# One more tile of a fused attention and feed-forward kernel takes its first products by a seven-product block scheme

## The chip, the cores and the metric

The kernel runs on one core of one Trainium2 chip. The metric is device time in microseconds (us), the median of several executions. A core has five engines that work side by side, each through its own list of instructions: PE (matmul; PEld is its weight load), DVE (vector), ACT (scalar), POOL (GpSimd) and SP (which here only issues DMAs). Engines wait for one another through semaphores.

## The reference

```
r = maximum(x, 0); phi(x) = concat(r * cos, r * sin)      # q and k, position s of 576
kv = k_p^T v;  z = sum_s k_p;  attn = (q_p kv) / (q_p z + 1e-6)     # 8 batches, 8 heads, D = 64
x = attn as (4608, 512)
h = ((x @ w1) * (x @ w2)) @ w3                              # w1, w2: 512 x 1024
out = h @ w_out                                              # 4608 x 512
```

The kernel first forms w3 @ w_out once (`w34b`, 1024 x 512), so each tile of x needs x @ w1, x @ w2, their product abT and abT @ w34b.

## The kernel before

Attention runs by batch b (0 to 7) and chunk c (0 to 4: four of 128 positions, one of 64). The feed-forward runs by tile t (0 to 8) of 512 tokens; a tile's `xT` is filled by DMA transposes of finished chunks. What stands where is written out by hand in `PLAN`: each line is split at its semicolons and the steps are issued in that order, so every engine's instruction order follows from it. The steps that matter here:

- `f t`: the next piece of tile t's products (generator `ffn_groups`, L700, or `fast_units`, L832); `o t`: the next piece of abT @ w34b of a tile in `FAST`.
- `n b c`: the eight matmuls of a chunk's numerator and denominator (L603); `d b c`: its division on DVE (a reciprocal, L624, and a product, L625), into a tile `xblk`; `xd b c`: the DMA transpose on SP's queue that takes `xblk` to `xT`.
- `q`, `k b c n`: features, the cosine part on DVE (L517), the sine part for n heads on ACT (L522) and the rest on DVE (L525); `qd b c`: the DMA transpose of q's features, on SP's queue; `v b c`: a copy on DVE, ACT or POOL; `kv b`: 40 matmuls; `l`, `lg`, `lx`: loads, the last two gated.
- `tf i`: weight sum i; `xs t i`: sum i of blocks of x (L830); `h t p`: the product of two finished blocks (L889); `s t i`: sum i of blocks of abT (L1007).

Three ways lead through a tile. Tiles 0 and 1 do eight block products in both stages. Tiles in `SEVEN` (2 to 6) form x @ w1 and x @ w2 plainly, 64 matmuls of 256 columns and 32 of 512 on PE, copy one of the two on ACT (`asb`) and multiply on DVE (L762, L778); then abT @ w34b comes in seven chained block products (`seven_products`, L1009). Tiles in `FAST` (7 and 8) take x @ w1 and x @ w2 too by seven chained block products, since [w1 w2] is a 2 x 2 block matrix W11 W12 / W21 W22: 112 matmuls of 256 columns, with sums t1 to t4 of the weights and s1 to s4 of the tile. Each of four column groups then needs four copies on ACT (L862, L866, L869, L876) and three operations on DVE (L872, L880, L883), and two products more make the second half (L889):

```
for p, m in ((0, 4), (0, 2), (0, 5), (1, 1), (0, 3), (1, 6), (1, 7), (1, 2), (1, 4), (1, 5), (1, 3)):
    step(p, m)
    yield
```

Product 7 takes t3 and s3, product 6 t2 and s2, product 4 t4, product 3 s4. A product that is added to a bank waits for the copy or sum that reads the bank before it. The seven products of the second stage are chained in the same way: the block sums L1026 and the copies L1029 read a bank before it is written on.

Of the kernel before, what the change touches and what calls it, by code (L numbers as in the profile page):

```python
# [137 lines left out]
f 3; q 5 0 0; lx 6 q 0; lg 6 q 1; k 5 3 8
f 3; n 4 2; lg 6 k 0; xd 3 2; d 4 2 A; l 6 k 1; l 6 v 1; xd 3 3; q 5 1 4; xd 4 0; xd 4 1; xd 4 2
f 3  # L140
f 3; q 5 3 8
# [4 lines left out]
f 4
f 3; n 4 3; k 5 2 8; k 5 0 0; qd 5 0
f 4
f 3; q 5 4 0; qd 5 4; v 6 0 G; d 4 3 A
f 4; v 6 1 G  # L150
f 4; lx 7 k 0
f 4; n 4 4
# [2 lines left out]
f 4; xd 4 3
f 4; q 5 2 8; d 4 4 V; qd 5 1; qd 5 3
f 4; kv 5
f 4; qd 5 2; n 5 0; xd 4 4; k 6 0 0; d 5 0 V; lg 7 k 1; n 5 4; v 6 3 A
# [89 lines left out]
f 8
f 8
f 8; h 8 0 V; s 8 3 V  # L250
f 8
f 8
f 8; h 8 1 V
o 8
f 8; s 8 2 V; s 8 4 V; s 8 1 V; ss; ss
o 8
# [66 lines left out]
def kernel(  # L323
# [483 lines left out]
    W11, W12, W21, W22 = (w[:, ts(r, 2), :] for r in range(2) for w in (w1b, w2b))

    def ffn_weight_sum(i, on):

# [2 lines left out]
        on.tensor_tensor(out=out, in0=a, in1=b, op=ALU.subtract)
# [7 lines left out]
    def x_sum(t, i, on):

        if t not in xsums:
            flat = va_bufs[t % 2 ^ 1][:].rearrange("p c h e -> p (c h e)")
# [5 lines left out]
        on.tensor_tensor(out=out, in0=a, in1=b, op=op)  # L830

    def fast_units(t):  # L832

        (s1, s2, s3, s4), (t1, t2, t3, t4) = xsums[t], wsum
# [7 lines left out]
        (m7, u1), (c11, c21, c22) = spare["f32"], spare["bf16"]  # L842
        x, y, z = {}, {}, {}

        def product(into, u, m, first=True):
            w, a = factors[m]
            for i in range(2):
                for kc in range(2):
                    nc.tensor.matmul(into[:, ts(i, 256)], lhsT=w[:, kc, ts(2 * u + i, 128)], rhs=a[:, kc, :],  # L849
                                     start=(first and i == 0 and kc == 0), stop=(i == 1 and kc == 1),  # L850
                                     skip_group_check=not first)

        def step(p, m, js=(0, 1)):
            if m == 1:
                for bank in (x, y):
                    for j in range(2):
                        bank[2 * p + j] = keep_bank()
            for j in js:
                u = 2 * p + j
                if m == 1:  # L860
                    product(x[u], u, 1)
                    nc.scalar.copy(out=y[u][:, :], in_=x[u][:, :])  # L862
                elif m == 7:
# [2 lines left out]
                    nc.scalar.copy(out=m7[:, j], in_=z[u][:, :])  # L866
                elif m == 6:
                    product(x[u], u, 6, False)
                    nc.scalar.copy(out=u1[:, j], in_=x[u][:, :])  # L869
                elif m == 4:  # L870
# [1 line left out]
                    nc.vector.tensor_tensor(out=c21[:, j], in0=z[u][:, :], in1=u1[:, j], op=ALU.add)  # L872
# [337 lines left out]
```

## Time and profile before

| | |
|---|---|
| median of 3 runs | 241.46 us (240.49 to 241.84) |
| profiled execution, its own time | 240.19 us |
| its span, first to last instruction | 238.4 us |
| mean granted clock of PE | 1.000 |
| POOL busy | 83.1 us, 35% of the span |

The span is what the profile's times count from (0 to 238.4); some 1.8 us of the execution's time lie outside it. "Busy" is the time in which an engine had an instruction at work. In the timeline each row gives start, length, engine, line of the program, operation, what is written and read, and in brackets how long the engine had sat idle and who released it. A matmul row lasts longer than the step to the next one, since matmuls overlap; the step from start to start is what a matmul costs.

### The profile page before, as it was taken

How to read it: one execution, taken by the hardware profiler on the slowest of the kernel's cores; microseconds unless marked ns; L12 is line 12 of the kernel's file. 1: busy time of each engine (PE TensorE's matmuls, PEld its weight loads, DVE VectorE, ACT ScalarE, POOL GpSimd, SP SyncE). 2: the span in 40 equal slices, each digit the busy share in tenths (PEclk: the TensorE clock that was granted, in tenths of full speed). 3: DMA queues.
4: the chain of work that ended last, by engine and by line, in shares of the span. 5: the costliest groups of instructions: out<-in, count | busy, mean ns of one | idle time of the engine just before them, and what ended most of it. 6: DMA issues, size and time to landing. Idle time of an engine off the chain costs nothing.

```text
span 238.4 us, 5947 instructions
## 1 busy us (share of the span) xinstructions
PE 231.4 (97%) x2281; PEld 169.4 (71%) x2300; DVE 189.0 (79%) x443; ACT 129.2 (54%) x240; POOL 83.1 (35%) x152
## 2 busy tenths in 40 slices
PE   7999999999999999999999999999999999999993
PEld 2579544475974486698668867975997598988872
DVE  6874595958878955997789598887998997895682
ACT  2754314587754933776563356636646347645730
POOL 8763788780900423030560050400211050660000
PEclk9999999999999999999999999999999999999999
DMA  7999999999999999999899999694676954899934
GB/s 192 196 197 198 160 195 182 197 196 196 180 189 132 156 140 222 168 138 219 68 160 173 160 157 158 93 215 94 89 146 122 171 103 149 193 283 298 235 110 166
DMA packets 86141, 40.51 MB, mean 170 GB/s; under 512 B 49632, under 2 KB 83424, under 8 KB 86112
## 3 DMA queue, kind: packets, MB, share of 16 engines
q0 software_dynamic: 38672, 23.60, 67.5%
q1 hardware_dynamic: 47152, 16.33, 40.4%
q8 instruction: 18, 0.29, 0.5%
q10 hardware_dynamic: 288, 0.20, 0.3%
q14 instruction: 11, 0.09, 0.1%
HBM read 38.80 MB, written 9.44 MB: 202 GB/s over the span
## 4 chain that ended last, share of the span: by engine, by line
PE 73%; DMA 18%; POOL 5%; issue 1%; DVE 1%; POOLq 0%
PE ffnps L709 34%; PE ffnps L1018 13%; PE ffnps L849 7%; DMA kf<-in_k_dram 6%; DMA w2b<-in_moe_w_dram 5%; DMA qs<-in_q_dram 4%; PE pnum L609 4%; PE pnum L574 3%; PE ffnmore L849 3%; PE ffnps L793 3%; DMA early<-in_moe_w_dram 2%; PE ffnmore L1018 2%; POOL early L424 2%; PE ffnps L950 1%; PE ffnmore L940 1%
## 5 line engine op out<-in xcount | busy, mean ns | idle before, releaser
L709 PE MATMUL ffnps<-xT,w2b 128*128 128x256 bf16 (+2 forms) x367 | 59.7, 295 | 0.1
L709 PE MATMUL ffnps<-xT,w1b 128*128 128x256 bf16 (+2 forms) x358 | 58.8, 293 | 0.6 <-PE unread L476 0.2
L709 PEld LDWEIGHTS <-w1b 128*128 128x128 bf16 x368 | 33.4, 98 | 13.7 <-issue 0.8
L709 PEld LDWEIGHTS <-w2b 128*128 128x128 bf16 x368 | 33.3, 98 | 13.9
L772 ACT CAST asb<-ffnps 128x512 bf16<-128x512 f32 x28 | 16.4, 585 | 24.0 <-PE ffnps L709 22.2
L625 DVE TENSOR_TENSOR xblk<-pnum,den 128x512 bf16<-128x512 f32 (+1 forms) x38 | 26.2, 691 | 1.9
L436 POOL COPY seen<-asb 128x1 bf16<-128x1 bf16 x15 | 3.6, 237 | 54.8 <-ACT asb L772 34.6
L778 DVE TENSOR_TENSOR abT<-asb,ffnps 128x512 bf16<-128x512 bf16 x28 | 18.9, 678 | 3.7 <-PE ffnps L709 3.6
L762 DVE TENSOR_TENSOR abT<-asb,ffnps 128x512 bf16<-128x512 bf16 x20 | 13.7, 684 | 9.5 <-PE ffnps L709 9.2
L1018 PEld LDWEIGHTS <-abT 128*128 128x128 bf16 x192 | 18.4, 98 | 3.2 <-DVE abT L778 0.3
L755 ACT CAST asb<-ffnps 128x512 bf16<-128x512 f32 x20 | 11.7, 584 | 16.3 <-PE ffnps L709 14.8
L522 ACT ACTIVATE kp<-kf,sinv 128x512 bf16<-128x512 bf16 (+4 forms) x28 | 18.1, 679 | 0.6 <-DMA kf<-in_k_dram 0.6
L609 PEld LDWEIGHTS <-qpT 128*128 128x128 bf16 x320 | 14.5, 98 | 4.6 <-DVE xblk L625 0.8
L522 ACT ACTIVATE qp<-qs,sinv 128x512 bf16<-128x512 bf16 (+5 forms) x26 | 16.0, 623 | 3.2 <-DMA qs<-in_q_dram 1.5
L609 PE MATMUL pnum<-kvs,qpT 128*128 128x65 bf16 x304 | 15.2, 194 | 0.5 <-DVE xblk L625 0.3
L1018 PEld LDWEIGHTS <-s 128*128 128x128 bf16 x144 | 13.8, 98 | 1.9 <-DVE s L1007 0.3
L793 PE MATMUL ffnps<-w34b,abT 128*128 128x512 bf16 x60 | 14.9, 379 | 0.2
L517 DVE TENSOR_SCALAR kp<-kf,cosv 128x512 bf16<-128x512 bf16 (+1 forms) x40 | 14.1, 374 | 0.3 <-PE pnum L574 0.3
L538 POOL COPY va<-vs 128x512 bf16<-128x512 bf16 (+1 forms) x12 | 7.5, 638 | 19.4 <-DMA vs<-in_v_dram 19.4
L494 PE MATMUL ffnps<-early,turned 128*128 128x512 bf16 x62 | 14.2, 379 | 0.1
L517 DVE TENSOR_SCALAR qp<-qs,cosv 128x512 bf16<-128x512 bf16 (+1 forms) x34 | 12.8, 386 | 1.9 <-issue 0.8
L483 DVE STREAM_TRANSPOSE turned<-early 128x512 bf16<-128x512 bf16 (+1 forms) x12 | 9.9, 864 | 2.9 <-DMA early<-in_moe_w_dram 2.9
(170 smaller groups left out, 436.5 us busy)
## 6 DMA issues: line engine op xcount, KB each, us to landing
kf<-in_k_dram POOLq DMA_DIRECT2D x7, 320.0 KB, 8.0
early<-in_moe_w_dram POOLq DMA_DIRECT2D x16, 128.0 KB, 5.4
out_dram<-osb SPq DMA_DIRECT2D x8, 256.0 KB, 4.6
vs<-in_v_dram POOLq DMA_DIRECT2D x6, 320.0 KB, 6.8
kf<-in_k_dram POOLq DMA_DIRECT2D x7, 256.0 KB, 8.1
qs<-in_q_dram POOLq DMA_DIRECT2D x5, 320.0 KB, 9.1
qs<-in_q_dram POOLq DMA_DIRECT2D x6, 256.0 KB, 6.5
vs<-in_v_dram POOLq DMA_DIRECT2D x6, 256.0 KB, 7.9
```

Of the source, the lines that this page charges most:

```text
L494: nc.tensor.matmul(acc[:, :], lhsT=w3T[:, lc, :], rhs=woutb[:, lc, :], start=(lc == 0), stop=(lc == 7))
L517: nc.vector.tensor_scalar(out=dst[:R, c, :, 0:D], in0=rows[:R], scalar1=0.0, scalar2=cosv[:R, at:at + 1], op0=ALU.max, op1=ALU.mult)
L522: nc.scalar.activation(out=dst[:R, c, 0:n, D:F], in_=rows[:R, 0:n], func=ACTF.Relu, scale=sinv[:R, at:at + 1], bias=0.0)
L609: nc.tensor.matmul(nt[:, h // 4, ds((h % 4) * 65, 65)], lhsT=qpT[:, h, ds(at, 128)], rhs=kvs[:, h, :], start=True, stop=True)
L625: nc.vector.tensor_tensor(out=xblk[rows, g0:g0 + ng], in0=n4[:, :, :, 0:D], in1=den[rows, 0:ng].unsqueeze(3).to_broadcast([R, ng, 4, D]), ...
L709: nc.tensor.matmul(out, lhsT=w[:, kc, ts(jc, 128)], rhs=x[:, kc, tok], start=(first and kc == 0), stop=(kc == 3), skip_group_check=not first)
L762: nc.vector.tensor_mul(out=abT[:, ts(pair, 2), ts(half, 256)], in0=asb[:].rearrange("p (i n) -> p i n", i=2), in1=bT[:, :].rearrange("p (i ...
L772: nc.scalar.copy(out=asb[:], in_=aT[:, :])
L778: nc.vector.tensor_mul(out=abT[:, jc, :], in0=asb[:], in1=bT[:, :])
L793: nc.tensor.matmul(ops[:, :], lhsT=abT[:, jc, ts(ms, 128)], rhs=w34b[:, jc, :], start=(jc == 0), stop=(jc == 7))
L849: nc.tensor.matmul(into[:, ts(i, 256)], lhsT=w[:, kc, ts(2 * u + i, 128)], rhs=a[:, kc, :], start=(first and i == 0 and kc == 0), stop=(i ...
L1018: nc.tensor.matmul(into[:, ts(ms, 256)], lhsT=a[:, kc, ts(ms, 128)], rhs=b[:, kc, :], start=(first and ms == 0 and kc == 0), stop=(ms == 1 ...
```

## The change

Tile 6 goes from `SEVEN` to `FAST`. So x @ w1 and x @ w2 of tiles 6, 7 and 8 come by seven products. What goes with it:

- Weight sums t1 and t2 (in the buffers `turned`, as before) are made in tile 2. Sum t3 = W22 - W12 is now written over W12 in `w2b`, whose last reader is tile 5; t4 goes to a buffer of `qs`. Before, t3 and t4 went to the buffers of k's features.
- The copies of m7 and u1 (fp32) lie in `kf` and a buffer of `vs`, c21 and c22 in the tile's buffers s1 and s2, c11 in an `asb` tile; before they lay in `kf` and in the buffers of q's features.
- The block sums of x of a tile lie in `va0` for tiles 6 and 8, in `va1` for tile 7.
- The steps of batches 4 to 7 and of tiles 3 to 8 are placed anew, and several sine parts move from DVE to ACT (`q 5 0 8` for `q 5 0 0`).

```diff
-f 2; xd 2 3; lg 4 q 0
+f 2; tf 1 V; xd 2 3; lg 4 q 0
-f 2; l 4 q 1; qd 3 2
+f 2; tf 2 V; l 4 q 1; qd 3 2
...
+f 5; n 6 0; xd 5 2; n 6 4; d 6 0 A; d 6 4 A; v 7 0 A
 f 5
+f 5; lg 7 k 1; lg 7 v 1; n 6 2; d 6 2 A; xd 6 0; v 7 4 G; q 7 0 8; sg; xd 6 4
 f 5
+f 5; more
+f 5
+f 6; tf 3 V
+f 5; xs 6 1 V; xs 6 3 V; xs 6 2 V; qd 7 2; v 7 3 G; tf 4 V; qd 7 0; n 6 3; d 6 3 A; v 7 2 G; k 7 4 8
 f 6
+f 6; k 7 1 8; q 7 4 8; qd 7 4
+f 6; n 6 1; d 6 1 A; xs 6 4 V
 f 6
 f 6
+f 6; q 7 1 4; xd 6 2; sg; kv 7
+f 6; q 7 3 8; h 6 0 V; s 6 3 V
 f 6
 f 6
 f 6
 f 6
+f 6; n 7 4; d 7 4 A; h 6 1 V; qd 7 1
+o 6; s 6 2 V
+o 6
+f 6; s 6 1 V; qd 7 3; s 6 4 V; n 7 3; xd 6 1; gx 0; d 7 3 A
+o 6; sx; xd 6 3
+o 6
+o 6
+o 6; xd 7 4; n 7 2; xs 7 1 V; xs 7 3 V; xs 7 2 V; xs 7 4 V
+f 7; d 7 2 V
+o 6; xd 7 2; st
...
-SEVEN = (2, 3, 4, 5, 6)
-FAST = (7, 8)
-BY_HALF = {t: (1, 0) if t == 3 else (0, 1) for t in range(2, 7)}
+SEVEN = (2, 3, 4, 5)
+FAST = (6, 7, 8)
+BY_HALF = {t: (1, 0) if t == 3 else (0, 1) for t in range(2, 6)}
...
-    wsum += [kp_bufs[0][:, ts(i, 2)].rearrange("p c h f -> p (c h f)").rearrange("p (c j) -> p c j", c=2) for i in range(2)]
     W11, W12, W21, W22 = (w[:, ts(r, 2), :] for r in range(2) for w in (w1b, w2b))
+    wsum.append(W12)
...
+        if len(wsum) == 3:
+            flat = ld.tile([P, H, NCH, D], BF16, name="qs", bufs=NRQ)[:].rearrange("p h j d -> p (h j d)")
+            wsum.append(flat[:, 0:2048].rearrange("p (c j) -> p c j", c=2))
...
-            flat = va_bufs[t % 2 ^ 1][:].rearrange("p c h e -> p (c h e)")
+            flat = va_bufs[t % 2][:].rearrange("p c h e -> p (c h e)")
...
-            flat = kf[:, 0:2048].rearrange("p (n m) -> p n m", n=4)
-            spare["f32"] = [flat[:, 0:2], flat[:, 2:4]]
-            spare["bf16"] = [qp_bufs[0][:, c].rearrange("p h f -> p (h f)").rearrange("p (n m) -> p n m", n=2) for c in range(3)]
+            flat = ld.tile([P, H, NCH, D], BF16, name="vs", bufs=NRV)[:].rearrange("p h j d -> p (h j d)")
+            spare["f32"] = [x.rearrange("p (n m) -> p n m", n=2) for x in (kf[:, 0:1024], flat[:, 0:2048].bitcast(FP32))]
...
+        c21, c22 = (s[:].rearrange("p a m -> p (a m)").rearrange("p (n m) -> p n m", n=2) for s in s_of(t)[1:])
...
-                    nc.scalar.copy(out=c11[:, j], in_=y[u][:, :])
+                    c11[u] = fsb.tile([P, 512], BF16, name="asb")
+                    nc.scalar.copy(out=c11[u][:], in_=y[u][:, :])
```

Two places of DVE's order follow. The line numbers of the changed program are 3 lower up to L813 and 4 or 5 higher behind it (L1026 is L1031, L1007 is L1012, L830 is L834, L872 is L876).

The first place is DVE at the entry into the first tile whose products are chained. Before, this is tile 7: the division of a chunk of batch 7, the three block sums of tile 6's output, the block sums of x (`va`).

```order
L624 RECIPROCAL den<-den 128x8
L625 TENSOR_TENSOR xblk<-pnum,den 128x512
L1026 TENSOR_TENSOR early<-ffnps_410,early 128x2x256
L1026 TENSOR_TENSOR early<-ffnmore_3006,early 128x2x256
L1026 TENSOR_TENSOR early<-ffnmore_3005,early 128x2x256
L830 TENSOR_TENSOR va_94<-xT 128x512 x2
L830 TENSOR_TENSOR va_94<-va_94,xT 128x512
```

Now it is tile 6, behind the output of tile 5 (`q0f`):

```order
L1031 TENSOR_TENSOR q0f<-ffnps_410,q0f 128x2x256
L621 RECIPROCAL den<-den 128x8
L622 TENSOR_TENSOR xblk<-pnum,den 128x512
L514 TENSOR_SCALAR qp_93<-qs,cosv 128x8x64
L1031 TENSOR_TENSOR q0f<-ffnps_411,q0f 128x2x256
L1031 TENSOR_TENSOR q0f<-ffnps_408,q0f 128x2x256
L813 TENSOR_TENSOR w2b<-w2b 128x2048
L834 TENSOR_TENSOR va_94<-xT 128x512 x2
L834 TENSOR_TENSOR va_94<-va_94,xT 128x512
L813 TENSOR_TENSOR qs<-w1b,turned 128x2048
L621 RECIPROCAL den<-den 128x8
L622 TENSOR_TENSOR xblk<-pnum,den 128x512
```

The weight sum t3 (`w2b<-w2b`) now stands between the block sums of the output and the sums of x, and t4 right behind these; before, both had been made while tile 6 was at work.

The second place is DVE where tile 6 passes from its products to its output. Before, the products of `asb` and a bank (L778) alternate with the sums of abT (L1007); t4 is among them.

```order
L778 TENSOR_TENSOR abT<-asb,ffnps_408 128x512
L623 TENSOR_SCALAR den<-pnum 64x8
L624 RECIPROCAL den<-den 64x8
L625 TENSOR_TENSOR xblk<-pnum,den 64x512
L813 TENSOR_TENSOR kp_92<-w1b,turned 128x2048
L778 TENSOR_TENSOR abT<-asb,ffnps_409 128x512
L1007 TENSOR_TENSOR s_2735<-abT,s_2734 128x512
L1007 TENSOR_TENSOR abT<-abT 128x2x256
L1007 TENSOR_TENSOR s_2736<-abT,s_2735 128x1024
```

Now (L876 makes c21, L885 c22, L894 their product, L888 the product of c11 and a bank, L1012 the sums of abT):

```order
L876 TENSOR_TENSOR s_2764<-ffnmore_2750,vs 128x512
L876 TENSOR_TENSOR s_2764<-ffnmore_2751,vs 128x512
L885 TENSOR_TENSOR s_2765<-ffnps_411,kf 128x512
L885 TENSOR_TENSOR s_2765<-ffnps_408,kf 128x512
L621 RECIPROCAL den<-den 64x8
L622 TENSOR_TENSOR xblk<-pnum,den 64x512
L894 TENSOR_TENSOR abT<-s_2764,s_2765 128x4x256
L1012 TENSOR_TENSOR s_2764<-abT,s_2763 128x1024
L888 TENSOR_TENSOR abT<-asb,ffnps_411 128x2x256
L888 TENSOR_TENSOR abT<-asb,ffnps_408 128x2x256
L1012 TENSOR_TENSOR abT<-abT 128x4x256
L1012 TENSOR_TENSOR s_2765<-abT,s_2764 128x1024
```

The sum that the output's third product reads (`s_2764<-abT,s_2763`) has the four operations c21 and c22, a division and the product of c21 and c22 ahead of it, where before it had one product of `asb` and a bank.

More of the change, by code (lines that the diff above doesn't have):

```diff
@@ L132 @@
 f 3; lg 5 q 0; lt 5 q 1; kv 4; k 5 1; d 3 3 V; k 5 4; v 5 4 V
-f 3; qd 4 3
-f 3; v 5 1 G; n 4 0; d 4 0 A; n 4 1; d 4 1 A; lg 6 v 0
-f 3
-f 3
-f 3
[L138 to L141, printed above, removed]
-f 3
-f 3
+f 3; qd 4 3; v 5 1 V; xd 3 3
+f 3; n 4 0; d 4 0 V; n 4 1; d 4 1 V
+f 3
+f 3
+f 3; xd 3 2
+f 3; lg 6 v 0; n 4 2; n 4 3; d 4 2 A; q 5 0 8; xd 4 1; q 5 3 8
+f 3
+f 3; xd 4 0; lx 6 q 0; lg 6 q 1
+f 3; l 6 v 1; lg 6 k 0; v 6 1 G
+f 3
+f 3
+f 3; q 5 4 8; qd 5 4; q 5 1 8
+f 3; d 4 3 V
+f 4; xd 4 3
 f 3
+f 4; l 6 k 1; n 4 4; k 5 2 8
 f 3
[L146 to L152, printed above, removed]
-f 4
-f 4
[L155 to L158, printed above, removed]
-f 4
-f 4; k 6 1 0
-f 4; d 5 4 A
-f 4; k 6 4 8
+f 4; q 5 2 0
+f 4
+f 4
+f 4; k 5 0 2
+f 4
+f 4; d 4 4 V; qd 5 0
+f 4; k 5 3 6
+f 4
+f 4
+f 4; v 6 4 V; kv 5; k 6 0 8
+f 4; qd 5 3; xd 4 2; n 5 0; d 5 0 A; lx 7 k 0; n 5 4
+f 4; v 6 3 V
+f 4; qd 5 2; qd 5 1; d 5 4 A
 f 4
@@ L225 @@
 f 7; h 7 0 V
-f 7; sx; ss; st
-f 7
-f 7; n 7 1; d 7 1 V; s 7 3 V; xd 7 1; ss; sg; ss
-f 7
-f 7
-f 7
-f 7; st; h 7 1 V; s 7 2 V
-o 7; xs 8 1 V; s 7 1 V
-f 7; xs 8 3 V
-o 7
-o 7
-o 7; s 7 4 V
-f 8; ss; sg; ss
+f 7
+f 7
+f 7; s 7 3 V; n 7 1; d 7 1 V
+f 7; xd 7 1
+f 7; ss
+f 7
+f 7; h 7 1 V; s 7 2 V; xs 8 1 V; sg; s 7 1 V
+o 7
+f 7; ss; s 7 4 V
+o 7
+o 7; st
+o 7
+o 7
 o 7
+f 8; xs 8 3 V; ss; xs 8 2 V; sg
 o 7
-o 7; xs 8 2 V; xs 8 4 V
+f 8
+f 8
+f 8; xs 8 4 V
 f 8
@@ L244 @@
 f 8
+f 8; s 8 3 V
+f 8
+f 8; ss
+f 8; ss; ss; h 8 0 V
 f 8
 f 8
+o 8; h 8 1 V
 f 8
[L248 to L256, printed above, removed]
+o 8; s 8 2 V; s 8 4 V; s 8 1 V
 o 8
@@ L838, in fast_units @@
         if "f32" not in spare:
-            flat = kf[:, 0:2048].rearrange("p (n m) -> p n m", n=4)
-            spare["f32"] = [flat[:, 0:2], flat[:, 2:4]]
-            spare["bf16"] = [qp_bufs[0][:, c].rearrange("p h f -> p (h f)").rearrange("p (n m) -> p n m", n=2) for c in range(3)]
-        (m7, u1), (c11, c21, c22) = spare["f32"], spare["bf16"]
-        x, y, z = {}, {}, {}
+            flat = ld.tile([P, H, NCH, D], BF16, name="vs", bufs=NRV)[:].rearrange("p h j d -> p (h j d)")
+            spare["f32"] = [x.rearrange("p (n m) -> p n m", n=2) for x in (kf[:, 0:1024], flat[:, 0:2048].bitcast(FP32))]
+        m7, u1 = spare["f32"]
+        c21, c22 = (s[:].rearrange("p a m -> p (a m)").rearrange("p (n m) -> p n m", n=2) for s in s_of(t)[1:])
+        x, y, z, c11 = {}, {}, {}, {}
         def product(into, u, m, first=True):
@@ L883, in step @@
                     nc.vector.tensor_mul(out=abT[:, ts(u, 2), 0:256],
-                                         in0=c11[:, j].rearrange("p (i m) -> p i m", i=2),
+                                         in0=c11[u][:].rearrange("p (i m) -> p i m", i=2),
                                          in1=x[u][:, :].rearrange("p (i m) -> p i m", i=2))
```

61 lines of the change are left out of this document (20 added, 41 removed).

## The prediction

> **What bounds the kernel now.** I read the page's first part, then the busy time by stretches, then the chain of waits, then the rows of PE and DVE where tile 5's output passes into tile 6 and tile 6's into tile 7.
>
> ```profile
> PE 231.4 (97%) x2281; PEld 169.4 (71%) x2300; DVE 189.0 (79%) x443; ACT 129.2 (54%) x240; POOL 83.1 (35%) x152
> ```
>
> PE works 97% of the span, so fewer matmuls should shorten it. But 79% for DVE is a mean. The stretches from 60 us on show where it isn't spread evenly (columns as in the first row):
>
> ```profile
> core 0: us, PE busy (x) PEld busy (x) DVE busy (x) ACT busy (x) POOL busy (x), PEclk, DMA share, GB/s
> 60.00:139.07 79.07, 78.70 (x819) 58.67 (x823) 64.24 (x157) 46.25 (x86) 24.74 (x49) 1.00 1.27 163
> 166.65:196.98 30.33, 30.23 (x320) 24.45 (x321) 27.73 (x61) 15.08 (x31) 6.59 (x14) 1.00 0.73 128
> ```
>
> From 60 to 139 us DVE works 64.24 of 79.07 us. From 166.65 to 196.98, the stretch in which tile 6 runs, it works 27.73 of 30.33 (91%) and PE 30.23. PE bounds it, but DVE has 2.6 us to spare there, no more. ACT (15.08) and POOL (6.59) have half of the stretch free, and the clock is full (1.00).
>
> **What PE saves.** Three pieces of the chain of waits and four rows of PE price its work.
>
> ```profile
> 160.11 1.27 PE pnum L574 x40
> 162.50 4.32 PE ffnps L709 x20
> 173.70 0.87 PE ffnps L709 x8
> ```
> ```profile
> 166.65 1.04 PE L1018 MATMUL ffnps<-w34b,abT 128*128 128x256 bf16 x8
> 170.66 0.42 PE L609 MATMUL pnum<-kvs,qpT 128*128 128x65 bf16 x8
> 170.92 1.03 PE L1018 MATMUL ffnps<-early,abT 128*128 128x256 bf16 x8
> 196.98 0.60 PE L849 MATMUL ffnmore<-va,kp 128*128 128x256 bf16 x4
> ```
>
> Eight matmuls of 256 columns take 0.87 us (0.873 from start to start in PE's rows), one of 512 columns 4.32 / 20 = 0.216, the eight of a chunk of attention 0.26 (170.66 to 170.92), a `kv` 1.27. Tile 6's first products cost 8 x 0.873 + 32 x 0.216 = 13.89 us before and 14 x 0.873 = 12.22 after: **-1.67 us**. Its second stage keeps its 56 matmuls, and loads and transposes keep their number. Without any wait the stretch from 166.65 to 196.98 would shrink from 30.33 to 28.66 us.
>
> **What DVE has to do in it.** These are the rows of DVE that price the steps; what counts is the time from one start to the next.
>
> ```profile
> 166.92 0.69 DVE L778 TENSOR_TENSOR abT<-asb,ffnps 128x512 bf16<-128x512 bf16 x1 [0.43 <-PE ffnps L709]
> 167.64 0.42 DVE L1007 TENSOR_TENSOR s<-abT,s 128x512 bf16<-128x512 bf16 x1
> 167.99 0.41 DVE L1007 TENSOR_TENSOR abT<-abT 128x512 bf16<-128x512 bf16 x1
> 168.32 0.68 DVE L1007 TENSOR_TENSOR s<-abT,s 128x1024 bf16<-128x1024 bf16 x1
> 168.92 0.19 DVE L624 RECIPROCAL den<-den 128x8 f32<-128x8 f32 x1
> ...
> 169.82 0.68 DVE L1026 TENSOR_TENSOR q0f<-ffnps,q0f 128x512 f32<-128x512 f32 x1
> ...
> 172.90 0.68 DVE L1026 TENSOR_TENSOR q0f<-ffnps,q0f 128x512 f32<-128x512 f32 x1
> 173.50 0.34 DVE L517 TENSOR_SCALAR qp<-qs,cosv 128x512 bf16<-128x512 bf16 x1
> 173.76 0.31 DVE L525 TENSOR_SCALAR qp<-qs,sinv 128x384 bf16<-128x384 bf16 x1
> ...
> 189.39 1.20 DVE L813 TENSOR_TENSOR kp<-w1b,turned 128x2048 bf16<-128x2048 bf16 x1
> 190.52 0.67 DVE L778 TENSOR_TENSOR abT<-asb,ffnps 128x512 bf16<-128x512 bf16 x1
> ...
> 195.78 0.75 DVE L830 TENSOR_TENSOR va<-xT 128x512 bf16<-128x512 bf16 x2
> 196.45 0.42 DVE L830 TENSOR_TENSOR va<-va,xT 128x512 bf16<-128x512 bf16 x1
> 196.78 0.16 DVE L623 TENSOR_SCALAR den<-pnum 128x8 f32<-128x8 f32 x1
> ...
> 199.42 1.29 DVE L872 TENSOR_TENSOR qp<-ffnmore,kf 128x512 bf16<-128x512 f32 x2 [1.18 <-ACT kf L866]
> ```
>
> So a product of `asb` and a bank steps 0.72, sums of abT 0.34 and 0.60, a division 0.90 (168.92 to 169.82), a block sum of the output 0.60, a cosine feature 0.26, a weight sum 1.13 (189.39 to 190.52), a sum of x 0.34 (196.45 to 196.78 is 0.33), and c21 or c22 0.60 a half (two took 0.60 + 0.69 = 1.29).
>
> Between the last product of tile 5 (the row at 166.92) and the third sum of x of tile 7, the changed order holds: that product 0.72; tile 5's last sums 1.28; 7 divisions 6.30; 6 block sums 3.60; 7 features 1.82; t3 and t4 2.26; 6 sums of x 2.04; 12 halves of c21, c22 and the products with c11 7.20; the two products of c21 and c22 1.20; sums of abT 2.60. That is 29.0 us, against 28.66 on PE. **DVE becomes the bound of the stretch** by a little, and every place where it has to wait for PE adds to it. I follow the two engines through three places.
>
> **Place 1, the entry into tile 6.** PE from 166.65: eight blocks (6.98) and four chunks of attention (1.04) take it to 174.67, where product 7 wants t3 and s3. DVE from 166.92: 0.72 + 0.34 + 0.34 + 0.60 to 168.92; three divisions (2.70), one feature (0.26), three block sums (1.80) to 173.68; t3 1.13 to 174.81; the first sums of x 0.34, and s3 with its 0.42 to 175.57. Product 7 begins at about 175.62: **+0.95**. Nothing in the trace shows this wait itself. It is nothing if DVE comes out 0.95 earlier, and near 2 if DVE waits once more for a bank as it does at 166.92 (0.43) or a division comes late; I take the sum.
>
> **Place 2, the third product of tile 6's output.** PE from 175.62: fifteen blocks (13.10), `kv` (1.27), three chunks (0.78) to 190.77. The sum it needs (`s_2764`) hangs on the first half of product 4 of the second group, ready on PE after ten and a half blocks, `kv` and one chunk: 175.62 + 9.17 + 1.27 + 0.26 = 186.32. DVE began its product 0.27 after PE's next start (166.65, 166.92), so 186.59; four halves 2.40, a division 0.90, the product of c21 and c22 0.60, then the sum, which reads what was just written, 0.1 + 0.69: 191.28. **+0.5**, bounds 0 (DVE can take the division behind) to 1.1 (another division ahead). The next sums make another +0.1.
>
> **Place 3, the entry into tile 7.** DVE from 191.28: the two products with c11 1.20, two sums of abT 1.20, a division 0.90, three block sums 1.80, s1 0.34, s3 0.42: 197.14. PE, with the two waits and 1.67 less, wants it at 196.98 - 1.67 + 1.55 = 196.86. **+0.3**. So product 7 of tile 7 begins at about 197.15, where it began at 196.98; the work behind is the same on every engine.
>
> ```profile
> 208.09 1.04 PE L1018 MATMUL ffnps<-w34b,abT 128*128 128x256 bf16 x8
> 208.99 1.19 PE L849 MATMUL ffnmore<-va,w2b 128*128 128x256 bf16 x8
> 210.02 2.07 PE L1018 MATMUL ffnps<-early,s 128*128 128x256 bf16 x16
> 211.93 1.04 PE L1018 MATMUL ffnps<-early,abT 128*128 128x256 bf16 x8
> ```
>
> Here PE stands still in the first passage out of a chained tile: 0.90 for 0.87, 1.03 for 0.87, 1.91 for 1.75, together 0.35 us. With division and sums placed anew I take 0.2 of it as gone (bounds 0 and 0.35).
>
> **What costs nothing.** t1 and t2 move to tile 2, where DVE waits for PE ahead of each product:
>
> ```profile
> 88.66 0.69 DVE L762 TENSOR_TENSOR abT<-asb,ffnps 128x512 bf16<-128x512 bf16 x1 [1.06 <-PE ffnps L709]
> 90.41 0.69 DVE L762 TENSOR_TENSOR abT<-asb,ffnps 128x512 bf16<-128x512 bf16 x1 [1.06 <-PE ffnps L709]
> 92.41 0.69 DVE L762 TENSOR_TENSOR abT<-asb,ffnps 128x512 bf16<-128x512 bf16 x1 [1.32 <-PE ffnps L709]
> ```
>
> A sum of 1.13 fills one such gap; if a product came late it would be by tenths. ACT trades four casts for eight more copies at that tile and some sines; at 0.6 each that is under 5 us in a stretch in which it has 15 free. The buffers change no count of loads.
>
> **The sum.** -1.67 + 0.95 + 0.5 + 0.1 + 0.3 - 0.2 = -0.02 us: the profiled execution would go from 240.19 to 240.2. It lies 1.27 below the median of the runs, 241.46, so I add that: **241.4 us**. About 0.5% (1.2 us) is what a measurement of this kernel can tell from no change, and the whole saving is 0.7%.
>
> **The rivals.** *Faster, 0.25.* The waits at places 1 to 3 don't arise, since DVE comes to 166.92 without its backlog or puts the divisions into gaps. For it: ACT takes over sines, and DVE's 29.0 us exceed PE's 28.66 by only 0.34. Then -1.1 to -1.67, and up to 0.2 more: 239.6 to 240.3, say 240.0. Against it: t3 can't be earlier, as it is written over W12, which tile 5 reads to the end.
>
> *Slower, 0.13: a transpose that lands late.* The features of batch 7's chunk 3 (`qd 7 3`) are now done late in tile 6: their last part stands just ahead of the second group's first products on DVE, by the sums above at about 184.9, and chunk `n 7 3` stands on PE at about 190.5, just ahead of the third output product, which waits until 191.3 anyway.
>
> ```profile
> DMA to landing us min/median/max: 2.7/5.5/10.1
> ```
>
> This is the row of the q transposes, L546. At the median, 184.95 + 5.5 = 190.4, it is hidden. From 6.3 us on it holds PE one for one, with all of the output behind it: at the longest 195.05, +3.8; at 7.8 us +1.5, which is 242.9. That is slower than before.
>
> *Slower, 0.07: the last 64 rows of batch 7's k.* Their load now waits for a buffer until about 166.5, and ACT's sine of them stands ahead of the copies of m7 and u1.
>
> ```profile
> kf<-in_k_dram POOLq DMA_DIRECT2D x1, 64.0 KB, 7.0
> ```
>
> Issued at 167.2, at 7.0 us it is there at 174.2, before ACT wants it at about 175.4. Beyond 8.2 us it delays the copies, and product 6 waits for their bank; 2 us more are 242 to 243.4.
>
> *DVE by full durations, 0.01.* If each operation began only when the one before it had ended, seventeen steps from 166.92 to place 1 would each cost some 0.08 more (0.68 for 0.60): +1.3, 242.8. The row at 172.90 speaks against it: 0.68 long, the next starts at 173.50. [...]
>
> *No change, 0.54:* the forecast.
>
> **How the numbers follow.** Faster by over 0.5% is the first rival, 0.25. Slower by over 0.5% is the three others, 0.21. The rest is 0.54. The range runs from the first rival's end, 239.5, to the late transpose at its typical price and the low end of the late load, 243.0; longer landings, a tenth at most, are left out.
>
> **What would show it.** Right: a wait of about 1 us on PE ahead of product 7 of tile 6 (matmuls from `va` and the sum in `w2b`), with DVE named; about 0.5 ahead of the third product of tile 6's output; DVE busy for nearly all of the 30 us; product 7 of tile 7 near 197; no wait for `qpT`. Wrong: PE without idle time there and tile 7 at 195.5; or a wait for a DMA ahead of a chunk of attention; or a wait outside 160 to 200 us, where I expect none that is new.

## The result, and the profile after

| | before | changed |
|---|---|---|
| median of 20 runs of each | 240.77 us | 241.94 us |
| ratio | | 1.0064 (95%: 1.0038 to 1.0090) |
| profiled execution, its own time | 240.19 us | 242.57 us |
| its span | 238.4 us | 240.8 us |

The changed kernel is slower by 0.64%, about 1.5 us by the ratio, where the forecast was no change. Some executions are disturbed as a whole (of the repeat r0 below, six of 13, its profiled one of 246.04 us among them); the ratios leave them out, the medians don't. The page's first part, after:

```profile
PE 231.3 (96%) x2316; PEld 170.9 (71%) x2316; DVE 192.7 (80%) x446; ACT 135.0 (56%) x252; POOL 84.8 (35%) x155
```

Its busy times can't be compared with those of before to a per cent: there 19 of the matmul records were missing (2281 beside 2300 weight loads), here none (2316 of each). The stretch of tile 6, from the start of tile 5's output to product 7 of tile 7, shows it (columns as in the prediction's windows):

```profile
167.42:199.38 31.96, 29.60 (x337) 25.98 (x336) 29.76 (x58) 18.90 (x40) 8.53 (x18) 1.00 0.74 144
199.38:240.80 41.42, 37.59 (x340) 31.75 (x339) 30.24 (x58) 21.16 (x42) 7.92 (x17) 1.00 0.69 192
```

It lasts 31.96 us, where it lasted 30.33 (166.65 to 196.98). What follows lasts 41.42 in both (238.4 - 196.98, 240.8 - 199.38). Another 0.77 us lie ahead of the stretch (it begins at 167.42, not 166.65); they come from a wait of 0.78 us for a transpose at 104.84 us, to which I return. PE's rows of the stretch, with their waits:

```profile
167.42 1.04 PE L1023 MATMUL ffnps<-w34b,abT 128*128 128x256 bf16 x8
...
173.70 1.04 PE L853 MATMUL ffnmore<-xT,w1b 128*128 128x256 bf16 x8
176.03 1.03 PE L1023 MATMUL ffnps<-w34b,s 128*128 128x256 bf16 x8 [1.30 <-DVE q0f L1031]
176.90 0.42 PE L606 MATMUL pnum<-kvs,qpT 128*128 128x65 bf16 x8
177.83 0.60 PE L853 MATMUL ffnps<-va,w2b 128*128 128x256 bf16 x4 [0.51 <-DVE va L834]
...
193.62 1.05 PE L1023 MATMUL ffnps<-early,s 128*128 128x256 bf16 x8 [0.41 <-DVE s L1012]
...
198.31 1.04 PE L1023 MATMUL ffnps<-w34b,s 128*128 128x256 bf16 x8
199.38 0.60 PE L853 MATMUL ffnmore<-va,w2b 128*128 128x256 bf16 x4
```

Product 7 of tile 6 starts at 177.83, 10.41 us behind the start of the stretch; the prediction had 175.62 - 166.65 = 8.97. From there to product 7 of tile 7 it is 21.55, where the prediction had 197.15 - 175.62 = 21.53. So the whole difference in the stretch, 1.44 us, arose at place 1. DVE's rows there, and POOL's beside them:

```profile
172.72 0.69 DVE L622 TENSOR_TENSOR xblk<-pnum,den 128x512 bf16<-128x512 f32 x1
173.33 1.45 DVE L514 TENSOR_SCALAR qp<-qs,cosv 128x512 bf16<-128x512 bf16 x1
174.70 1.27 DVE L1031 TENSOR_TENSOR q0f<-ffnps,q0f 128x512 f32<-128x512 f32 x2
175.90 1.21 DVE L813 TENSOR_TENSOR w2b<-w2b 128x2048 bf16<-128x2048 bf16 x1
177.03 0.75 DVE L834 TENSOR_TENSOR va<-xT 128x512 bf16<-128x512 bf16 x2
177.70 0.41 DVE L834 TENSOR_TENSOR va<-va,xT 128x512 bf16<-128x512 bf16 x1
```
```profile
172.88 0.58 POOL L684 DMA_DIRECT2D out_dram<-early  x1
173.45 1.18 POOL L535 COPY va<-vs 128x512 bf16<-128x512 bf16 x2
```

The cosine feature at 173.33, which I took at 0.26 from start to start, holds DVE for 1.37 us. No wait stands beside it: it has started, and it is slow. It lasts until POOL's two copies of v, 173.45 to 174.63, are over. Behind it stand tile 5's last two block sums, t3 and the sums of x, so PE waits twice: 1.30 us for a block sum whose bank it wants to write on, and 0.51 for s3.

The trace of before had shown the like, outside of the rows that the prediction shows. Its DVE and POOL near 77 us:

```profile
77.33 1.32 DVE L517 TENSOR_SCALAR qp<-qs,cosv 128x512 bf16<-128x512 bf16 x2
78.58 0.95 DVE L517 TENSOR_SCALAR kp<-kf,cosv 64x512 bf16<-64x512 bf16 x2
```
```profile
77.75 1.37 POOL L538 COPY va<-vs 128x512 bf16<-128x512 bf16 x2
```

Two features there cost 1.25 us from start to start, 0.62 each, not 0.26, beside two copies on POOL.

**Theory 1:** a feature on DVE is held up while POOL copies, and that is what the prediction lacked. Rivals: the transposes on SP's queue hold it up; the wait for a transpose at 104.84 us, behind the weight sums moved to tile 2, is the loss (theory 2); DVE's whole work is the bound of the stretch, wherever its steps stand (theory 3).

### The profile page after: what moved, and what is told of

Same layout as the page of the kernel before. It is cut to its first block, busy times and chain, and to the rows that moved or that the text cites. A ratio compares the mean times of both kernels' runs of the same rounds, so it can differ in the third digit from the quotient of the medians.

```text
span 240.8 us, 6012 instructions
## 1 busy us (share of the span) xinstructions
PE 231.3 (96%) x2316; PEld 170.9 (71%) x2316; DVE 192.7 (80%) x446; ACT 135.0 (56%) x252; POOL 84.8 (35%) x155
## 5 line engine op out<-in xcount | busy, mean ns | idle before, releaser
L706 PE MATMUL ffnps<-xT,w1b 128*128 128x256 bf16 (+2 forms) x320 | 51.5, 294 | 1.0 <-DMA xT<-xblk 0.8
L706 PE MATMUL ffnps<-xT,w2b 128*128 128x256 bf16 (+2 forms) x320 | 51.5, 294 | 0.0
L706 PEld LDWEIGHTS <-w1b 128*128 128x128 bf16 x320 | 28.7, 98 | 13.1 <-DMA xT<-xblk 1.1
L706 PEld LDWEIGHTS <-w2b 128*128 128x128 bf16 x320 | 28.8, 98 | 11.9
L769 ACT CAST asb<-ffnps 128x512 bf16<-128x512 f32 x24 | 14.0, 585 | 18.2 <-PE ffnps L706 18.1
L519 ACT ACTIVATE kp<-kf,sinv 128x512 bf16<-128x512 bf16 (+5 forms) x33 | 20.8, 656 | 1.3 <-DMA kf<-in_k_dram 1.3
L519 ACT ACTIVATE qp<-qs,sinv 128x512 bf16<-128x512 bf16 (+4 forms) x29 | 18.1, 643 | 5.2 <-DMA qpT<-qp 2.1
L775 DVE TENSOR_TENSOR abT<-asb,ffnps 128x512 bf16<-128x512 bf16 x24 | 16.1, 678 | 5.6 <-PE ffnps L706 4.5
L535 POOL COPY va<-vs 128x512 bf16<-128x512 bf16 (+1 forms) x15 | 9.8, 660 | 26.1 <-DMA vs<-in_v_dram 26.1
L759 DVE TENSOR_TENSOR abT<-asb,ffnps 128x512 bf16<-128x512 bf16 x16 | 11.0, 686 | 7.3 <-PE ffnps L706 6.1
L1023 PEld LDWEIGHTS <-s 128*128 128x128 bf16 x144 | 13.7, 98 | 3.8 <-issue 1.5
L752 ACT CAST asb<-ffnps 128x512 bf16<-128x512 f32 x16 | 9.4, 585 | 10.1 <-PE ffnps L706 9.9
L1023 PE MATMUL ffnps<-early,s 128*128 128x256 bf16 x96 | 12.4, 273 | 0.4 <-DVE s L1012 0.4
```

The lines of the kernel that those rows point to most:

```text
L519: nc.scalar.activation(out=dst[:R, c, 0:n, D:F], in_=rows[:R, 0:n], func=ACTF.Relu, scale=sinv[:R, at:at + 1], bias=0.0)
L706: nc.tensor.matmul(out, lhsT=w[:, kc, ts(jc, 128)], rhs=x[:, kc, tok], start=(first and kc == 0), stop=(kc == 3), skip_group_check=not first)
L759: nc.vector.tensor_mul(out=abT[:, ts(pair, 2), ts(half, 256)], in0=asb[:].rearrange("p (i n) -> p i n", i=2), in1=bT[:, :].rearrange("p (i ...
L769: nc.scalar.copy(out=asb[:], in_=aT[:, :])
L775: nc.vector.tensor_mul(out=abT[:, jc, :], in0=asb[:], in1=bT[:, :])
L1023: nc.tensor.matmul(into[:, ts(ms, 256)], lhsT=a[:, kc, ts(ms, 128)], rhs=b[:, kc, :], start=(first and ms == 0 and kc == 0), stop=(ms == 1 ...
```

## The experiments

All are the changed kernel with the edits named (where a run builds on another one, its heading says so and the edit is shown against that one), each compared with the kernel before on the same chip. The kernel before was timed anew for each group of runs, with medians from 239.97 to 240.35 us beside r0 to r10, so runs are compared by their ratios and not by their medians. A is the start of tile 5's output, B product 7 of tile 6, C product 7 of tile 7, in the profiled execution, in us:

| run | A to B | B to C | median | ratio to before (95%) |
|---|---|---|---|---|
| before | | A to C 30.33 | 240.77 | |
| changed | 10.41 | 21.55 | 241.94 | 1.0064 (1.0038 to 1.0090) |
| r0_changed_again | 9.72 | 21.55 | 242.92 | 1.0055 (1.0018 to 1.0091) |
| r1_v_on_act | 9.30 | 21.56 | 240.85 | 1.0018 (0.9995 to 1.0041) |
| r2_feature_later | 9.05 | 21.60 | 240.22 | 0.9993 (0.9971 to 1.0015) |
| r4_t3_early | 10.17 | 21.99 | 241.65 | 1.0052 (1.0020 to 1.0085) |
| r5_feature_and_t3 | 8.37 | 21.99 | 240.14 | 0.9997 (0.9971 to 1.0022) |
| r6_division_behind | 8.37 | 22.20 | 240.81 | 1.0018 (0.9988 to 1.0048) |
| r7_t4_early | 9.02 | 22.00 | 241.25 | 1.0048 (1.0022 to 1.0073) |
| r8_sine_later | 9.02 | 21.72 | 240.25 | 0.9997 (0.9976 to 1.0018) |
| r9_division_ahead | 8.37 | 21.27 | 239.84 | 0.9967 (0.9936 to 0.9998) |
| r10_copies_elsewhere | 9.05 | 22.00 | 241.28 | 1.0043 (1.0011 to 1.0076) |

A ratio also moves by some thousandths for reasons outside of A to C (r7 and r8 differ by 0.28 us there and by 0.005, or 1.2 us, in the ratio), so the mechanisms are read from the rows, and the ratios only tell which side a run is on.

**The changed kernel again**, no edit.

> The changed kernel once more, as it is, to have it beside the experiments on the same chip. Theory 1 (a cosine feature on DVE at 173.33 us takes 1.45 us instead of 0.34, since POOL copies at the same time, and tile 6 begins later by that): the same feature is long again (over 1.2 us), ratio to the kernel before 1.004 to 1.009. Theory 2 (the wait of 0.78 us for a transpose into xT at 104.84 us is what makes the profiled run slow, through the weight sums that are now made in tile 2): this wait is there again, 0.5 us or more. If it is an accident of the one execution, it is not there, and the span is nearer to 240 than to 240.8 us.

It is slower than before once more, 1.0055. But the feature took 0.75 us here and not over 1.2, so that part of the expectation failed:

```profile
177.50 0.75 DVE L514 TENSOR_SCALAR qp<-qs,cosv 128x512 bf16<-128x512 bf16 x1
```
```profile
177.42 1.30 POOL L535 COPY va<-vs 128x512 bf16<-128x512 bf16 x2
```

It began behind the start of the first copy and ended at 178.25, while the second was still at work. It holds DVE for 0.67 us (to 178.17), 0.41 more than 0.26, and A to B is 9.72. So how much the feature loses differs from one execution to the next: 1.11 us in the first profiled one, 0.41 in this one.

The wait at 104.84 isn't there; this execution has another one, of 3.82 us at 105.88 for a copy on ACT, which no other run has. Of the ten executions of the changed kernel and its variants that are profiled below, one has the wait at 104.84 again: r9, the fastest by its median, with 0.50 us. Theory 2 falls: the weight sums of tile 2 stand in all of them, and the wait comes and goes.

**The copies of v on ACT.**

```diff
-f 5
+f 5; v 7 3 A; v 7 2 A
 f 6; tf 3 V
-f 5; xs 6 1 V; xs 6 3 V; xs 6 2 V; qd 7 2; v 7 3 G; tf 4 V; qd 7 0; n 6 3; d 6 3 A; v 7 2 G; k 7 4 8
+f 5; xs 6 1 V; xs 6 3 V; xs 6 2 V; qd 7 2; tf 4 V; qd 7 0; n 6 3; d 6 3 A; k 7 4 8
```

> The changed kernel with the copies of v of batch 7, chunks 2 and 3, on ACT just ahead of tile 6, no longer on POOL. Theory 1 (DVE and POOL hinder one another): the feature at 173 us is back to about 0.35 us, DVE's chain in front of product 7 of tile 6 gets 1.1 us shorter, that product begins about 10.4 - 1.1 = 9.3 us behind the start of tile 5's output, and the time falls by about 1.1 us: ratio 1.000 to 1.003. Rival (the feature is long because the transposes on SP's queue, which start at 173.28, read and write the memory at the same time): the feature stays above 1.2 us and the ratio at 1.004 to 1.009. Second rival (ACT, which gets 1.2 us of copies more, becomes late for m7 and u1): the feature is short, but the ratio is not.

DVE's rows of this run at the same place:

```profile
172.52 0.34 DVE L514 TENSOR_SCALAR qp<-qs,cosv 128x512 bf16<-128x512 bf16 x1
172.78 1.28 DVE L1031 TENSOR_TENSOR q0f<-ffnps,q0f 128x512 f32<-128x512 f32 x2
173.97 1.22 DVE L813 TENSOR_TENSOR w2b<-w2b 128x2048 bf16<-128x2048 bf16 x1
```

The feature is back to 0.34 us, 0.26 from start to start, A to B fell by 1.11 (by 0.42 against r0), and the ratio to 1.0018. The transposes still run beside it (from 172.47), so they are not the cause. The wait for the block sum went from 1.30 to 0.19; the 0.51 for s3, behind t3, stayed.

**The feature behind t4**, POOL's copies where they were.

```diff
-f 5; lg 7 k 1; lg 7 v 1; n 6 2; d 6 2 A; xd 6 0; v 7 4 G; q 7 0 8; sg; xd 6 4
+f 5; lg 7 k 1; lg 7 v 1; n 6 2; d 6 2 A; xd 6 0; v 7 4 G; qs 7 0 8; sg; xd 6 4
...
-f 5; xs 6 1 V; xs 6 3 V; xs 6 2 V; qd 7 2; v 7 3 G; tf 4 V; qd 7 0; n 6 3; d 6 3 A; v 7 2 G; k 7 4 8
+f 5; xs 6 1 V; xs 6 3 V; xs 6 2 V; qd 7 2; v 7 3 G; tf 4 V; qc 7 0; qd 7 0; n 6 3; d 6 3 A; v 7 2 G; k 7 4 8
```

> The changed kernel with the cosine part of q of batch 7, chunk 0, behind the weight sum t4 instead of ahead of tile 5's last block sums; POOL's copies stay. Theory 1: the feature is short there (0.3 to 0.4 us, POOL has finished), DVE's chain in front of product 7 loses 1.37 us, time -1.1 to -1.4 us: ratio 0.998 to 1.003. Rival (transposes): the feature is long at its new place too, as the transposes run on for 9.67 us, but behind t4, so the time falls by as much; the two are told apart by its duration.

The feature takes 0.35 us at its new place (176.73), the copies run from 171.90 to 173.07 beside a division and block sums that keep their 0.69, and A to B falls to 9.05, by 1.36 (by 0.67 against r0). The ratio is 0.9993: the time that the prediction had computed, no change.

**t3 early.** A buffer of its own for t3 has no room in SBUF (r3: one of the pools needs 17 kb per partition, 13.7 are left), so r4 puts it over k of batch 6 in `kf`, and m7 over W12.

```diff
-    wsum.append(W12)
+    wsum.append(kf[:, 0:1024].bitcast(BF16).rearrange("p (c j) -> p c j", c=2))
...
-            spare["f32"] = [x.rearrange("p (n m) -> p n m", n=2) for x in (kf[:, 0:1024], flat[:, 0:2048].bitcast(FP32))]
+            spare["f32"] = [x.rearrange("p (n m) -> p n m", n=2) for x in (w2b[:, 0:2, :].rearrange("p c j -> p (c j)").bitcast(FP32), flat[:, 0:2048].bitcast(FP32))]
...
-f 5; v 7 1 G
+f 5; v 7 1 G; tf 3 V
...
-f 6; tf 3 V
+f 6
```

> The changed kernel with t3 in the buffer of k of batch 6 (free by then), made in the middle of tile 5, and the copy m7 in W12's place; the feature and POOL's copies stay where the change put them. Place 1 of the prediction (t3's 1.13 us stand in front of product 7): the wait of 0.51 us for s3 goes, the wait for the block sum (1.30 in the profiled run, 0.60 in the second) stays as it is ahead of t3; the rest of DVE's lead (0.6 us) takes away the 0.41 us of place 2. Time -0.5 to -1.1 us: ratio 1.001 to 1.005. Rival (DVE's whole work between tile 5's output and tile 7 is the bound, wherever its steps stand): t3 leaves that stretch, so the rival gives -1.13 from product 7 to product 7; a wait at place 2 or 3 that stays would show that one. If nothing changes, t3 was not on the path.

A miss by half: the 0.51 us for s3 went, and yet A to B fell by 0.24 only, for the feature took 1.88 us here, with POOL's store and both copies beside it:

```profile
172.15 1.88 DVE L514 TENSOR_SCALAR qp<-qs,cosv 128x512 bf16<-128x512 bf16 x1
```
```profile
172.13 0.58 POOL L684 DMA_DIRECT2D out_dram<-early  x1
172.70 1.18 POOL L535 COPY va<-vs 128x512 bf16<-128x512 bf16 x2
```

So much depends on how the two meet: 0.41, 1.11 and here 1.55 us more than 0.26 (1.81 from start to start). And B to C grew by 0.44, with a new wait of 0.34 us for the copy of m7: the time won at the entry was lost again behind it. The ratio, 1.0052, lies just above the range expected.

**Both**, the edits of r2 and r4.

> Both: the feature behind t4 and t3 made early. If the two costs add up (1.1 to 1.4 us from the feature, 0.5 to 1.1 from t3), the time is 1.6 to 2.2 us below the changed kernel: ratio to the kernel before 0.994 to 0.998, faster than both. PE then goes from the start of tile 5's output to product 7 of tile 6 in 8.5 us or less (10.41 in the changed kernel, 9.05 with the feature alone; its own work there is 8.0). Rival (DVE is the bound of the whole stretch): the two waits go, but come back at places 2 and 3, and the ratio stays at 0.997 to 1.000.

A to B is 8.37, near PE's own 8.02. The two costs add up there: 1.36 and another 0.68. But B to C is 21.99. PE's rows name what is late next:

```profile
177.49 0.60 PE L853 MATMUL ffnps<-xT,qs 128*128 128x256 bf16 x4 [0.34 <-ACT w2b L870]
...
191.03 1.05 PE L1023 MATMUL ffnps<-early,s 128*128 128x256 bf16 x8 [0.42 <-DVE s L1012]
```

The copy of m7, behind ACT's sine of `k 7 4`, and place 2. The ratio, 0.9997, is not below that of the feature alone; it misses the range expected and lies in that of the rival. The next runs ask whether the whole work of DVE does this, or these two chains.

**The division of chunk 4 behind the sum**, on r5.

```diff
-f 6; n 7 4; d 7 4 A; h 6 1 V; qd 7 1
-o 6; s 6 2 V
+f 6; n 7 4; h 6 1 V; qd 7 1
+o 6; s 6 2 V; d 7 4 A
```

> The one before, and the division of batch 7's chunk 4 behind the sum that the third product of tile 6's output reads, not ahead of it (place 2, where the prediction named this as the way in which the wait would go). If that division makes the wait of 0.41 us: no wait there, and -0.2 to -0.4 us if DVE doesn't wait again at place 3. If the wait is gone already in the run before, no change here, or worse by up to 0.3 us at place 3, since the same 0.9 us of DVE still stand ahead of tile 7's sums.

```profile
192.37 0.42 PE L606 MATMUL pnum<-kvs,qpT 128*128 128x65 bf16 x8 [0.90 <-DVE xblk L622]
192.63 1.04 PE L1023 MATMUL ffnps<-early,s 128*128 128x256 bf16 x8
```

The wait for the sum is gone, and in its place the next chunk of attention waits 0.90 us, for the bank that this division frees. B to C is 22.20, 0.21 more. I had left that reader out of the expectation.

**t4 early too**, on r5.

```diff
-f 5; qd 6 4
+f 5; tf 3 V; qd 6 4
...
-f 5; v 7 1 G; tf 3 V
+f 5; v 7 1 G; tf 4 V
...
-f 5; xs 6 1 V; xs 6 3 V; xs 6 2 V; qd 7 2; v 7 3 G; tf 4 V; qc 7 0; qd 7 0; n 6 3; d 6 3 A; v 7 2 G; k 7 4 8
+f 5; xs 6 1 V; xs 6 3 V; xs 6 2 V; qd 7 2; v 7 3 G; qc 7 0; qd 7 0; n 6 3; d 6 3 A; v 7 2 G; k 7 4 8
```

> The feature behind t4's old place, and t3 and t4 both made in the middle of tile 5, one product of asb apart. This tells two theories apart on the half that is left. Theory 3 (DVE's whole work from tile 5's output to tile 7 is the bound: 29.0 us by the prediction, of which t4 and the feature's place don't matter, so that taking 0.5 us off the entry moved the wait to m7's copy and to place 2): with 1.13 us less on DVE in that stretch, the way from product 7 of tile 6 to product 7 of tile 7, 21.99 us in the run with both, falls to 21.2 us or less, the wait of 0.42 us at place 2 goes, and the time is 0.8 to 1.1 us below that run: ratio to the kernel before 0.993 to 0.998. Rival (ACT's copies of m7, 0.34 us late there, set the pace from then on): 21.99 stays, ratio 0.998 to 1.002. If the two sums hold up the products of tile 5 instead, a wait shows up on PE ahead of 166 us.

Theory 3 falls in its strict form. With 1.13 us less on DVE behind B, B to C is 22.00, the same two waits stand there with the same 0.34 and 0.42 us, and DVE itself now idles more (0.56, 0.24 and 0.36 us between 176 and 180, on ACT and PE). At the entry t4, squeezed in at 165.83, made tile 5's last products late on DVE, and PE waited for a division:

```profile
170.68 0.42 PE L606 MATMUL pnum<-kvs,qpT 128*128 128x65 bf16 x8 [0.75 <-DVE xblk L622]
```

A to B grew by 0.65 to 9.02. The ratio, 1.0048, lies above both ranges; the 0.65 us explain about half of the 1.2 us by which it exceeds that of r5, and the rest stays open.

**ACT's sine behind the copies of m7 and u1**, on r7 (`k 7 4 8` split into `kc 7 4` where it was and `ks 7 4` at the head of the second line behind it).

> As the run before, and ACT's sine of k of batch 7, chunk 4, behind the first copies of m7 and u1 instead of ahead of them. If ACT makes the wait of 0.34 us on PE behind product 7 of tile 6, it is gone, and with DVE no longer the bound the time falls by another 0.2 to 0.4 us: ratio 0.991 to 0.997. If DVE is still the bound, the wait goes and comes back at place 2 or 3, and the ratio is that of the run before within 0.001.

The 0.34 us are gone, and B to C is 21.72, 0.28 less; so this wait did not come back later. The ratio, 0.9997, misses the range expected; A to B is still 9.02.

**The division of chunk 4 ahead**, on r5 with the sine moved. With it the division's first step, `den`, goes from ACT to DVE (`V` for `A`).

```diff
-f 6
+f 6; n 7 4; d 7 4 V
...
-f 6; n 7 4; d 7 4 A; h 6 1 V; qd 7 1
+f 6; h 6 1 V; qd 7 1
```

> The feature behind t4's place and t3 early (t4 where the change has it), ACT's sine of k 7 4 behind the first copies of m7 and u1, and the numerator and division of batch 7's chunk 4 four products earlier, where DVE waits 0.62 us for PE. If the wait of 0.42 us at place 2 is the chain that the prediction set up there (a division between c22 and the product of c21 and c22), it goes now, and with it the 0.2 us at place 3: product 7 of tile 6 to product 7 of tile 7 in 20.7 to 21.1 us (21.99 with the division and the sine at their places), time 0.9 to 1.2 us below the kernel before: ratio 0.995 to 0.997. Rival (DVE's whole work is the bound): the wait comes back as a later one, 21.4 us or more, ratio 0.998 to 1.001.

```profile
190.73 0.42 PE L606 MATMUL pnum<-kvs,qpT 128*128 128x65 bf16 x8
191.11 1.05 PE L1023 MATMUL ffnps<-early,s 128*128 128x256 bf16 x8
...
195.80 1.04 PE L1023 MATMUL ffnps<-w34b,s 128*128 128x256 bf16 x8
196.87 0.60 PE L853 MATMUL ffnmore<-va,kf 128*128 128x256 bf16 x4
```

The chunk and the third product stand 0.38 apart, where the chunk alone takes 0.26: the wait at place 2 shrank to 0.12. Place 3 kept its 0.20 (1.07 from 195.80, for 0.87). B to C is 21.27, between the two expectations, and A to C is 29.64, the first below the 30.33 of before. The ratio is 0.9967, a third of a per cent below the kernel before. Its interval ends at 0.9998, so that it is faster than the kernel before is likely and not certain; the division's place and its `den` on DVE were not tried apart.

**The copies beside other features**, on r2, with POOL held back until the moved feature is done.

```diff
-f 5; xs 6 1 V; xs 6 3 V; xs 6 2 V; qd 7 2; v 7 3 G; tf 4 V; qc 7 0; qd 7 0; n 6 3; d 6 3 A; v 7 2 G; k 7 4 8
+f 5; xs 6 1 V; xs 6 3 V; xs 6 2 V; qd 7 2; tf 4 V; qc 7 0; gm; v 7 3 G; v 7 2 G; qd 7 0; n 6 3; d 6 3 A; k 7 4 8
...
+        "gm": lambda: gate(made[0]),
```

> The run with the feature behind t4, but POOL's copies of v of batch 7, chunks 2 and 3, held back until that feature is done, so that they run beside the next cosine features on DVE (k 7 4, k 7 1, q 7 4: 0.26 us each from start to start so far). Theory 1 (a feature of DVE that runs while POOL copies takes longer, whichever it is): one or two of these three take 0.6 us or more, together 0.5 to 1.2 us more than their 0.8, while the division beside the same copies stays at 0.69. Rival (something special to the first feature, such as its buffer): they stay at 0.26 to 0.35. The time moves by less than 0.5 us either way, as DVE has a little slack behind t4.

```profile
178.52 0.35 DVE L514 TENSOR_SCALAR qp<-qs,cosv 128x512 bf16<-128x512 bf16 x1
178.79 0.19 DVE L621 RECIPROCAL den<-den 128x8 f32<-128x8 f32 x1
179.08 0.69 DVE L622 TENSOR_TENSOR xblk<-pnum,den 128x512 bf16<-128x512 f32 x1
179.69 1.00 DVE L514 TENSOR_SCALAR kp<-kf,cosv 64x512 bf16<-64x512 bf16 x2
180.62 0.34 DVE L514 TENSOR_SCALAR qp<-qs,cosv 64x512 bf16<-64x512 bf16 x1
```
```profile
179.12 1.16 POOL L535 COPY va<-vs 128x512 bf16<-128x512 bf16 x2
```

The first feature is short, the division beside the copies keeps its 0.69, and the two features that meet the copies take 0.93 from start to start, where they took 0.52 in r2. The excess, 0.41, is a little below what I had expected, since the copies end at 180.28; the third feature, behind that, is short. B to C grew by 0.40. So it is whichever feature meets POOL, not the first one. PE seems to lose what DVE lost: its row that comes late, `kv` at 183.21, starts 0.15 behind the end of the division that began at 182.37, and so does the one of r2 (181.01, division from 180.17), though the profile puts its wait of 0.30 down to a copy on ACT. The median, which I had expected within 0.5 us of that of r2, is 1.06 above it; the stretch explains 0.40 of that, the rest stays open.

## Why the prediction was wrong

- **What PE saves:** right. A to C without waits was to be 28.66 us. In the changed kernel six steps of PE are longer than their price, by 0.26 (170.82), 1.46 (176.03), 0.67 (177.83), 0.07 (180.08), 0.58 (193.62) and 0.20 us (199.38); without these 3.24, its 31.96 are 28.72. In r9 such steps add up to 0.93 of its 29.64.
- **Place 1:** wrong, and this is the step that failed: "three divisions (2.70), one feature (0.26), three block sums (1.80)". The feature took 1.37, since the copies of `v 7 3` and `v 7 2` ran on POOL beside it; that is 1.11 of the 1.44 us, shown by the two runs that part them (r1: -1.11, r2: -1.36 with the feature's own 0.26). In the repeat (r0) the feature cost only 0.41 more than its 0.26, so 1.11 is the size in one execution; the cause is shown, its mean size is not. The divisions took 3.02 (169.70 to 171.83 for two, 0.89 for the third), 0.32 more. The upper bound, near 2, was about what PE lost (10.41 - 8.02 = 2.39, the first three of these steps), but for other reasons: I had worked out the wait ahead of product 7 and not the one for the block sum ahead of it. Nor did I ask what POOL does there, though POOL's copies of v were in the lines that the change moved. The wait of 0.95 that I had put on t3 turned out at 0.51 for s3; in r5 t3's removal took 0.68 off.
- **Place 2:** right in mechanism and size, 0.5 forecast and 0.58 measured (193.62 where 193.04 was wanted: 191.91 + 0.87 + 0.26). It is a local chain behind one half of product 4, as worked out there; r7 shows that it doesn't depend on DVE's load.
- **Place 3:** right, 0.3 forecast, 0.20 measured (198.31 + 0.87 = 199.18, start at 199.38).
- **"DVE becomes the bound of the stretch":** half right. DVE is busy for 29.76 of 31.96 us, but what PE waits for are three short chains. Taking 1.13 us off DVE's work (r7) changed nothing behind B; shortening the chains did (r8, r9).
- **The stalls of 0.35 us in tile 7's output:** I took 0.2 of it as gone; nothing went. C to the end is 41.42 us in both.
- **What costs nothing:** t1 and t2 in tile 2 were hidden, as far as the runs show; the wait at 104.84 comes and goes with them in place. But r1, r2, r5, r6 and r8 have a wait of 0.31 to 0.59 us on PE at 124 to 126 us, for a product of `asb` on DVE, that the kernel before doesn't show; the prediction expected no new one there, and its cause stays open.
- **The rivals:** no transpose of q and no load of k was late; PE's rows name neither in any run. The rival that came true, slower by a mechanism on POOL, was not on the list.

With what was measured put in, the forecast's sum becomes -0.02 + 1.44 + 0.2 = 1.6 us. The stretch lost 1.63 in the profiled executions, the timed runs 1.2 (medians) to 1.5 us (ratio); the 0.77 us ahead of the stretch come from the wait at 104.84, which two of the twelve profiled executions have.

## What to carry to other kernels

Before a step is priced by its row, look at what the other engine beside it does at the new place: the price of an operation in a profile holds for its neighbours there, and the rows of the same form with the longest duration show what else it can cost. And where one wait is taken away, list every reader of the same engine's order behind it (the bank that a division frees, the copy behind a sine): r4, r6 and r7 took one wait away and another one appeared, and only r9, which took out most of them, has an interval that ends below the kernel before.

## What the runs showed of the hardware

A cosine feature of q (DVE, bf16, from SBUF to SBUF) takes 0.33 to 0.35 us alone and up to 1.88 us beside POOL. Counted over the 12 profiled executions (before, changed, and the ten runs) from 60 us on, by what POOL did for at least 0.06 us of it (its copies under 0.4 us, such as those into `seen`, count as nothing):

```
POOL did nothing              268 features   0.33 to 0.35 us, median 0.34
POOL issued a DMA              34            0.33 to 0.58, median 0.35
POOL copied (0.4 us or more)   31            0.35 to 1.35, median 0.70
both                            3            0.70, 1.45, 1.88
```

The count leaves out the features of k, and these show that an issue alone can hold a feature up too. One of 64 rows took 0.71 to 0.72 us in the changed kernel and in all ten runs, beside nothing but the issue of a load on POOL; in the changed kernel:

```profile
154.42 0.72 DVE L514 TENSOR_SCALAR kp<-kf,cosv 64x512 bf16<-64x512 bf16 x1
```
```profile
154.14 0.88 POOL L393 DMA_DIRECT2D vs<-in_v_dram  x1
```

Operations of DVE with one input in a PSUM bank show nothing of it: divisions, block sums and products with `asb` take 0.67 to 0.70 us with a copy beside them and without. This agrees with the Trainium skill, "SBUF — State Buffer", section "Who interferes with whom": a DVE instruction with at most one SBUF input does not contend with GpSimd, as long as it runs outside of the modes with two ports, and `tensor_scalar`, the operation of the features, can run in such a mode, which takes the pair of ports that the two share; "Whoever issues first gets the shared pair for the whole instruction". No row names the mode of a feature; the durations fit it. Here the feature could lose more than one turn: in r4 it started beside a store's issue and ended when both copies behind that had ended (172.15 + 1.88 = 174.03; the copies from 172.70 to 173.88).
